# A 1022-operation schedule written out as a list of numbers is replaced by another list

## The chip, the cores and the metric

The kernel runs on one core of a Trainium2 chip. The metric is the device time of one execution in microseconds (us), as the median of several runs; less is better. The core has TensorE (matrix products and transposes, PE in the profile, with its weight loads as PEld), VectorE (DVE), ScalarE (ACT), GpSimd (POOL), SyncE (SP, which here only issues transfers) and 16 DMA engines that all queues share.

## The reference

Two blocks in sequence: an attention with polynomial features, and a wave-MLP over its output.

```python
# q, k, v: (4 batches, 4 heads, 1088 tokens, 32); S1, S2: (8, 32)
phi(x) = outer(S1 x, S2 x)                       # 64 features per token and head
kv  = einsum('bhsf,bhsd->bhfd', phi(k), v)
z   = sum over tokens of phi(k)
x   = (phi(q) kv) / (phi(q) z + 1e-6)            # then (B, H, S, D) -> (4, 1088, 128)
theta = x @ w_theta
zr, zi = x * cos(theta), x * sin(theta)
y   = w_tok_r @ zr + w_tok_i @ zi                # token mixing, 1088 x 1088, per batch
u   = x + y
out = u + relu(u @ w_ch)
```

The weights come as 64-bit words (w_tok, w_sq, S1, S2) and are made into 32-bit numbers on the chip; q, k and v come in 32 bits.

## The kernel before

**Stages.** For each of the four batches b there is a key side (load k and v; transposes kT, features kf, sums kv; a scale from the sum of squares; a rounding "grid" of the keys; key sums), a chain of small operations on the key sums (L.stage "chain", over batch 0, then 1, then 2 and 3 together) that gives the scaled sums in mv and mf, and a query side (load q; qscale; transposes qT scaled on the way; q0, the rounded part, and the rest). Then come, for each batch in order: `levels` (three groups of matmuls with a ScalarE copy of each, line 1002, and the denominator on VectorE), `num_g` for g = 0, 1, 2 (features of the queries on VectorE, transposed by TensorE at line 1064 and copied by ScalarE at 1068, or sent through DRAM for batches 2 and 3; matmul with kv; copy at 1078) and `theta_g` (theta on TensorE, sine and cosine on ScalarE at lines 1115 and 1117, products with x on VectorE, written to z). Below, "num1" is the three num stages of batch 1.

**Token mixing.** The 17 rows of w_tok, 128 x 1088 each, are loaded one by one (1088 KB, line 583), taken to 32 bits by two ScalarE operations (584 and 586) and two on VectorE (309 and 305), and stay in SBUF. Batches 0 and 1 are mixed directly, 17 x 3 matmuls each (128 x 384 per matmul: `mix0`, `mix1`). Batches 2 and 3 share seven products in Winograd's manner (m1 to m7; m5 is the first that needs theta of batch 3). Behind each the output stage adds x, multiplies by w_ch and stores.

**Joins.** A `join` is an accumulating transfer from SBUF to SBUF that GpSimd issues (line 319). In batches 2 and 3 it does the subtraction of a rounded half from the keys (ops 216 and 217 for batch 2, 252 and 253 for batch 3) and from the queries (329, 334); batches 0 and 1 use it in their output stage. The `small` operations of GpSimd, such as pbd, the block of key products that the scale chain's second matmul reads, stand in the same sequence.

**What sets the order.** Each operation is recorded by `op(engine, duration, function, writes, reads)` and gets a number. Nothing is scheduled when the kernel is built: `Layout.run` reads the sequence from the constant ORDER and each buffer's slot from PLACES, and `Layout.issue` walks it under a manual schedule:

```python
        self.order = [self.ops[int(i)] for i in ORDER.split()]
...
        for o in self.order:
            n, home = spins.get(o.i, 0), None
            if shared:
                for _ in range(n):
                    fill()
            for b in o.bufs:
                if b.ap is None:
                    raw = pools[b.cls](b.slot)
...
            o.fn()
```

Each engine, and the queue of each engine that issues transfers (SP, ACT, POOL), executes its own operations in the order in which ORDER names them. A buffer gets its slot at its first use, and waits there until the buffer that held the slot before has been read for the last time; the classes have 22 ("big"), 5 ("zs"), 6 ("hf") slots and so on. A wait on another engine is made by what reads what. SPINS says ahead of which operation `fill` issues how many filler matmuls of 128 x 384 into a PSUM buffer nobody reads (line 379); ten more are issued as operation 1. Operation 3 (line 384) computes one sine on ScalarE whose output, `warm`, nobody reads. The constants' durations in `op` are used for nothing in this kernel, since the order is given.

Matmuls go through `mm` (line 341), VectorE's two-input operations through `tt` (305), its scalar ones through `ts` (309), the combined ones through `stt` (312), so many operations share a line in the profile.

Of the kernel before, what the change touches and what calls it, by code (L numbers as in the profile page):

```python
# [26 lines left out]
TINY = 2.0**-60  # L27
UP = 256.0
ORDER = (
    "6 4 2 5 44 0 1 45 50 3 47 7 340 8 48 46 11 9 10 49 12 29 58 13 30 70 83 84 64 76 71 14 77 85 96 15 88 72 89 78 "  # L30
    "65 86 90 97 79 16 91 66 159 17 92 26 87 98 67 148 27 93 80 32 18 68 19 73 99 309 25 94 141 20 310 74 95 31 142 "
    "35 149 341 21 101 129 151 160 102 150 40 103 104 161 130 105 342 41 131 106 135 107 43 343 162 197 345 136 108 "
    "360 210 22 137 152 355 305 42 53 344 307 198 315 138 306 313 28 110 109 211 139 132 111 23 314 100 308 212 203 "
    "112 133 316 113 36 69 24 204 114 33 199 213 34 143 115 117 75 116 311 144 59 81 200 118 119 312 317 82 346 120 "
    "191 39 121 37 122 124 123 145 424 60 335 125 38 348 422 375 153 420 423 425 154 214 421 155 347 426 61 427 318 "
    "349 246 156 428 57 126 157 239 319 192 158 356 429 227 127 240 164 128 62 247 165 241 430 167 63 337 166 431 "
    "168 249 134 51 432 242 193 169 228 433 140 336 229 170 434 146 194 233 171 350 230 435 173 56 172 147 436 234 "
    "174 361 443 439 437 175 450 438 176 446 440 444 177 441 447 250 445 453 178 442 248 179 448 180 320 454 357 "
    "457 181 188 451 182 338 459 385 458 452 205 183 251 449 235 184 352 460 252 185 187 186 358 521 461 163 339 "
    "462 517 463 253 359 519 518 217 522 455 520 464 236 465 206 523 456 482 524 467 222 215 525 216 351 468 483 "  # L40
    "526 469 353 365 471 527 223 362 473 354 466 189 470 254 528 255 472 529 484 256 190 530 475 387 224 476 257 "
    "376 531 485 267 532 377 268 533 366 390 540 534 370 536 269 537 543 547 541 535 321 542 363 548 270 550 378 "
    "549 538 544 364 386 218 219 368 539 551 388 545 54 220 477 380 201 221 546 552 367 195 325 554 263 553 379 400 "
    "225 486 556 479 264 326 265 389 322 474 266 487 478 557 371 369 558 323 207 196 324 271 372 373 202 480 208 "
    "395 272 562 374 209 381 563 571 382 570 383 488 327 564 405 384 392 489 275 481 391 231 401 410 393 555 490 "
    "560 403 559 273 394 572 396 491 276 274 328 278 573 402 329 492 398 277 565 574 415 404 397 279 406 493 399 "
    "576 280 561 52 407 281 494 282 408 411 409 566 625 575 626 243 567 579 412 413 495 237 283 414 416 496 285 284 "
    "417 418 497 286 299 287 568 419 288 498 55 289 290 293 291 294 292 577 578 648 569 511 505 512 650 649 226 652 "
    "651 627 653 628 654 629 655 602 295 656 580 657 581 658 603 296 604 659 660 582 258 661 583 499 662 300 232 "
    "500 663 238 330 259 506 630 605 298 664 584 260 585 665 261 586 331 262 671 501 666 667 606 513 332 631 333 "  # L50
    "587 678 334 607 502 588 503 589 301 297 514 608 679 609 672 590 632 842 674 668 591 841 673 592 840 681 633 "
    "719 680 721 720 723 722 244 724 669 245 725 610 675 726 670 504 611 727 612 728 593 729 685 686 594 730 688 "
    "595 731 682 302 732 613 687 676 733 634 734 677 614 697 735 635 699 698 615 736 696 596 689 690 839 616 597 "
    "737 691 683 838 692 303 684 636 304 738 742 637 638 708 701 617 743 709 694 693 639 702 707 695 703 700 618 "
    "710 744 749 815 805 704 750 787 705 788 712 816 745 796 640 711 797 798 751 598 706 817 713 739 641 756 714 "
    "799 715 818 789 752 599 790 515 800 844 516 716 819 619 791 718 801 717 620 820 802 746 806 803 807 753 792 "
    "740 808 741 809 760 821 762 810 763 747 845 754 804 748 843 642 811 764 769 755 643 757 822 771 778 765 621 "
    "772 780 758 812 813 622 759 793 781 766 761 768 823 767 773 644 774 794 835 782 770 645 775 846 795 777 847 "
    "776 784 848 783 855 864 856 836 857 814 858 867 779 849 785 859 875 837 868 860 861 866 893 850 876 894 851 "
    "869 884 870 862 885 871 852 872 853 877 865 886 898 887 854 878 895 879 863 888 874 901 880 896 507 873 889 "  # L60
    "938 911 935 890 881 939 882 786 891 824 912 883 902 892 913 940 825 897 903 826 955 646 914 900 915 830 600 "
    "904 942 601 916 831 956 937 957 899 933 975 647 905 934 946 945 931 943 906 907 508 917 509 947 941 510 918 "
    "936 908 827 948 974 958 976 828 959 832 960 932 834 949 944 833 950 829 961 962 951 963 952 987 953 988 954 "
    "919 909 920 989 623 977 990 624 991 926 964 927 978 910 965 992 979 966 921 968 980 922 981 982 928 983 923 "
    "984 925 924 985 930 993 967 986 994 995 969 996 1007 971 929 1012 1013 1014 997 998 1015 999 1008 1000 1001 "
    "1009 1002 1003 1011 1010 1004 1005 970 1006 1016 1017 972 1018 1019 973 1020 1021 "
)
PLACES = (
    "7 0 1 5 0 10 17 16 14 0 15 5 6 15 18 0 10 3 5 0 11 5 3 4 3 6 3 6 2 2 8 4 4 0 5 12 0 6 12 4 12 4 6 5 4 7 1 5 8 "
    "5 10 8 4 4 1 5 9 0 8 8 5 2 0 4 1 6 10 1 0 1 1 4 2 4 0 3 1 4 6 0 4 3 5 1 3 2 21 2 10 6 5 8 3 5 4 3 5 12 4 1 0 2 "  # L70
    "3 2 9 2 0 6 4 4 1 2 1 0 4 2 3 7 3 5 3 3 5 2 4 4 4 6 4 5 4 1 3 5 0 2 3 5 2 0 8 12 1 7 0 7 0 11 4 2 12 7 2 5 5 8 "
    "3 5 3 1 5 4 2 8 12 3 0 3 2 4 3 5 0 1 0 2 4 4 1 7 4 5 3 0 3 19 0 11 13 2 11 8 2 5 16 0 10 2 1 4 7 4 1 11 0 10 3 "
    "4 1 5 3 15 17 1 20 14 1 17 20 3 0 1 4 15 6 0 18 0 1 10 18 3 10 9 0 10 0 6 1 5 6 0 12 2 0 0 0 6 6 2 2 1 4 4 1 0 "
    "7 0 1 6 5 4 1 4 1 4 5 0 0 3 6 5 0 2 4 4 1 3 7 2 0 3 5 4 21 1 21 4 3 4 2 5 7 2 3 7 4 7 1 2 5 2 2 4 7 2 7 1 3 2 "
    "5 4 1 1 0 2 5 3 4 5 4 0 5 5 0 5 2 3 4 6 12 1 3 1 1 2 4 0 2 3 2 3 3 6 5 0 4 1 2 3 0 0 0 6 3 0 0 3 0 7 10 1 10 3 "
    "1 2 2 0 3 1 1 6 3 0 4 5 0 0 3 5 4 6 4 2 6 5 2 5 3 2 0 5 4 15 7 1 6 5 7 0 5 0 1 5 1 6 7 2 6 0 1 7 3 3 1 4 2 5 2 "
)
SPINS = (
    "70:2 15:3 137:1 211:1 424:2 128:1 168:1 174:2 176:1 521:2 "
)  # L80
WARM = 0
SPLIT = ()
# [1330 lines left out]
```

## Time and profile before

| | us |
|---|---|
| device time, median of 3 runs (219.3 to 219.84) | 219.76 |
| span of the profiled execution (no other time of its own is given) | 217.4 |
| TensorE busy | 209.3 |
| of that, 27 fillers (L379) | 7.8 |
| VectorE busy | 181.2 |
| ScalarE busy | 111.2 |
| GpSimd busy | 22.2 |
| 17 rows of w_tok, 1088 KB each, from issue to landing (min, median, max) | 4.9, 7.0, 11.0 |

The page of the profile lists, in this order: busy time and share of each engine; the span in 40 slices of 5.4 us, with a digit per slice for the busy tenths; the DMA queues; the chain of work that ended last, by engine; and the costliest groups of instructions (line, engine, operation, output<-input, partitions x elements, count, then busy time and mean ns of one, then the idle time before them and what ended it). Stretches of the trace list busy time and number of instructions for PE, PEld, DVE, ACT and POOL, the granted clock of TensorE (1.00 is full), the mean share of the 16 DMA engines and GB/s. Timelines list start, duration, engine, line and operation; in brackets the idle time before and what ended it. A VectorE or ScalarE instruction can start before its neighbour has ended, so busy times can overlap.

### The profile page before, as it was taken

What the parts mean: (1) busy time and instruction counts of PE and PEld (TensorE: products, weight loads), DVE (VectorE), ACT (ScalarE), POOL (GpSimd) and SP (SyncE); (2) the same over time, 40 slices, a digit from 0 to 9 for tenths busy, and PEclk for the clock granted to TensorE, in tenths of its full rate; (3) what the DMA queues carried; (4) which work ended last, traced back from release to release, by engine and by line L of the source; (5) the groups of instructions that cost most, each with busy time, mean ns of one, the idle gap of its engine ahead of it and who ended that gap; (6) DMA issues with size and microseconds to landing.
All of it is one profiled execution on the core that took longest, in us unless ns stands there. A gap on an engine that the chain in (4) does not pass through costs nothing.

```text
span 217.4 us, 5063 instructions
## 1 busy us (share of the span) xinstructions
PE 209.3 (96%) x1998; PEld 154.3 (71%) x1998; DVE 181.2 (83%) x408; ACT 111.2 (51%) x214; POOL 22.2 (10%) x44
## 2 busy tenths in 40 slices
PE   7999899999999999999999999999999999999994
PEld 3987786686766686666766575667758788888883
DVE  4899999999999999999599839988138999996542
ACT  3998498899779999983322040354037400000010
POOL 2237000055000000100132000100101000000000
PEclk9999999999999999999999999999999999999998
DMA  5999996869979979894226998599911000045253
GB/s 153 429 406 340 425 399 203 333 224 271 267 276 361 361 264 380 219 198 126 33 36 102 222 137 199 105 156 151 231 78 32 0 0 0 3 66 89 36 79 75
DMA packets 52635, 40.58 MB, mean 187 GB/s; under 512 B 45444, under 2 KB 47108, under 8 KB 50436
## 3 DMA queue, kind: packets, MB, share of 16 engines
q1 hardware_dynamic: 35540, 33.71, 48.7%
q0 software_dynamic: 1728, 4.65, 10.5%
q10 hardware_dynamic: 15344, 1.90, 6.0%
q8 instruction: 15, 0.25, 0.5%
q14 instruction: 8, 0.07, 0.1%
HBM read 30.43 MB, written 5.18 MB: 164 GB/s over the span
## 4 chain that ended last, share of the span: by engine, by line
PE 72%; DVE 12%; ACT 8%; DMA 4%; ACTq 2%; issue 2%; SPq 1%
PE ps L341 66%; DMA big<-q_l 2%; DVE lv L305 2%; PE ps L1064 2%; ACTq L333 2%; PE ps L1098 1%; DMA fx<-g 1%; DVE g L305 1%; DVE big L305 1%; PE ps L967 1%; ACT big L584 1%; ACT big L937 1%; DVE hf L309 1%; DVE zs L305 1%; ACT g L1068 1%
## 5 line engine op out<-in xcount | busy, mean ns | idle before, releaser
L341 PE MATMUL ps<-big,zs 128*128 128x384 f32 (+4 forms) x398 | 109.7, 424 | 0.4 <-DVE zs L305 0.4
L341 PEld LDWEIGHTS ps<-big,zs 128*128 128x128 f32 x398 | 71.4, 190 | 30.3 <-issue 2.6
L1201 ACT COPY g<-ps 128x128 f32<-128x128 f32 (+1 forms) x3 | 0.9, 301 | 42.5 <-PE ps L1193 42.5
L305 DVE CUSTOM_DVE_ANT_0 big<-big,big 128x2176 uint16<-128x2176 uint16 x17 | 21.8, 1287 | 0.4 <-ACT big L586 0.2
L584 ACT ACTIVATE big<-zs 128x1088 f32<-128x1088 f32 x17 | 20.9, 1235 | 2.1 <-DMA zs<-w_tok 1.2
L586 ACT ACTIVATE big<-zs 128x1088 int32<-128x1088 uint32 (+1 forms) x18 | 21.3, 1184 | 0.1
L341 PE MATMUL ps<-big,big 128*64 128x64 f32 (+2 forms) x208 | 20.6, 276 | 0.0
L341 PEld LDWEIGHTS ps<-big,big 128*64 128x64 f32 (+1 forms) x208 | 16.5, 154 | 2.9 <-issue 0.2
L305 DVE TENSOR_TENSOR big<-big,big 128x544 f32<-128x544 f32 x24 | 16.7, 712 | 0.0
L1002 ACT COPY lv<-ps 128x480 f32<-128x480 f32 x12 | 6.3, 563 | 14.2 <-PE ps L341 14.2
L312 DVE SCALAR_TENSOR_TENSOR g<-g,ps 128x384 f32<-128x384 f32 x12 | 6.6, 548 | 8.1 <-ACT g L1111 8.1
L1078 ACT COPY big<-ps 128x384 f32<-128x384 f32 x12 | 5.9, 489 | 14.0 <-PE ps L341 8.3
L309 DVE TENSOR_SCALAR big<-big 128x1088 int32<-128x1088 int32 x17 | 12.2, 724 | 0.6 <-ACT big L584 0.5
L341 PEld LDWEIGHTS ps<-w,big 128*128 128x128 f32 x80 | 10.6, 192 | 2.3 <-ACT g L1068 0.6
L319 POOL DMA_DIRECT2D big<-hf x6 | 5.4, 957 | 63.3 <-DVE g L312 33.8
L319 POOL DMA_DIRECT2D g<-big x6 | 5.2, 920 | 64.8 <-ACT g L1179 34.7
L341 PE MATMUL ps<-w,big 128*128 128x128 f32 x80 | 11.8, 280 | 0.0
L305 DVE TENSOR_TENSOR g<-lv 128x768 f32<-128x768 f32 x12 | 11.2, 945 | 0.0
L341 PE MATMUL ps<-g,sm 128*64 128x384 f32 x48 | 10.1, 507 | 0.2 <-ACT big L1078 0.2
L305 DVE TENSOR_TENSOR zs<-ps,g 128x768 f32<-128x768 f32 (+2 forms) x15 | 9.4, 632 | 1.0 <-PE ps L1098 0.9
L341 PEld LDWEIGHTS <-hf 128*64 128x64 f16 (+1 forms) x288 | 7.7, 110 | 2.9 <-issue 1.7
L379 PE MATMUL ps<-idle 128*128 128x384 bf16 x27 | 7.8, 400 | 1.3 <-POOL idle L381 1.3
(194 smaller groups left out, 336.6 us busy)
## 6 DMA issues: line engine op xcount, KB each, us to landing
zs<-w_tok SPq DMA_DIRECT2D x17, 1088.0 KB, 7.0
big<-k_l SPq DMA_DIRECT2D x6, 576.0 KB, 6.6
big<-hf POOLq DMA_DIRECT2D x6, 576.0 KB, 6.0
big<-v_l SPq DMA_DIRECT2D x4, 576.0 KB, 7.0
g<-fq SPq DMA_DIRECT2D x6, 384.0 KB, 5.2
big<-q_l SPq DMA_DIRECT2D x3, 576.0 KB, 5.1
fq<-g SPq DMA_DIRECT2D x12, 96.0 KB, 4.0
fq<-g ACTq DMA_DIRECT2D x12, 96.0 KB, 4.1
```

Of the source, the lines that this page charges most:

```text
L305: eng.tensor_tensor(out=o, in0=a, in1=b, op=f)
L309: (eng or V).tensor_scalar(out=o, in0=a, scalar1=s1, scalar2=s2, op0=op0, **kw)
L312: (eng or V).scalar_tensor_tensor(out=o, in0=a, scalar=s, in1=b, op0=op0, op1=op1)
L319: op("G", 0.9, lambda: G.dma_start(dst(), src(), accum_op=ALU.add), w, r, fly=fly)
L333: E.dma_start(there().rearrange("(a i) (x b j) -> b i x a j", a=nf, b=nf, j=SQ)[f], blocks()[f * SQ:(f + 1) * SQ].rearrange("i (x a j) -> ...
L341: T.matmul(o, lhs, rhs, start=start, stop=stop, skip_group_check=True)
L379: T.matmul(nowhere() if home is None else view(home, (GW,), F32), idle()[:, 0:P], idle(), start=True, stop=True, skip_group_check=True)
L584: op("A", 0.22 + n * 0.0009, lambda: A.activation(dfn(), words_of(raw(), n)[1].bitcast(F32), AF.Prelu, scale=2.0**-112, alpha=-(2.0**32)), ...
L586: op("A", 0.22 + n * 0.0009, lambda: A.activation(stp(), words_of(raw(), n)[0].bitcast(U32), AF.Copy, scale=2.0**-29), [stp], [raw])
L1002: op("A", act(480), lambda g=g, lp=lp: A.copy(lv().rearrange("p l (c n) -> p l c n", n=HR)[:, :, g * GC:(g + 1) * GC], lp().rearrange("p c ...
L1064: T.transpose(tr()[:, i * P:(i + 1) * P], qp()[:, i * H + 2 * n:i * H + 2 * n + 2].rearrange("p h i j -> p (h i j)"), ident())
L1078: op("A", act(GW), lambda g=g, xp=xp: A.copy(xt()[:, g * GW:(g + 1) * GW], xp()), cells(xt, g * GW, (g + 1) * GW), [xp])
```

## The change

Three constants change and no function does. ORDER names the same 1022 operations in another sequence; 25 of them keep their place. PLACES gives 357 of 419 buffers another slot. SPINS asks for 9 fillers in six places where it asked for 16 in ten. The file is two lines shorter, so a line of the new kernel has a number two lower than here. In numbers that the prediction uses, places counted from 0: operation 3 moves from 9 to 370; the joins 217, 216, 252, 253 from 309, 325, 293, 305 to 93, 109, 135, 163; VectorE's operation of the second group of num1 (540) from 366 to 397. Operation 58 is the load of w2, 0 and 1 are the fillers' buffer and the first ten fillers, 2 writes the constants, 5 and 6 load the S matrices.

```diff
--- before.py
+++ after.py
@@ -27,56 +27,54 @@
 TINY = 2.0**-60
 UP = 256.0
 ORDER = (
-    "6 4 2 5 44 0 1 45 50 3 47 7 340 8 48 46 11 9 10 49 12 29 58 13 30 70 83 84 64 76 71 14 77 85 96 15 88 72 89 78 "
-    "65 86 90 97 79 16 91 66 159 17 92 26 87 98 67 148 27 93 80 32 18 68 19 73 99 309 25 94 141 20 310 74 95 31 142 "
-    "35 149 341 21 101 129 151 160 102 150 40 103 104 161 130 105 342 41 131 106 135 107 43 343 162 197 345 136 108 "
-    "360 210 22 137 152 355 305 42 53 344 307 198 315 138 306 313 28 110 109 211 139 132 111 23 314 100 308 212 203 "
-    "112 133 316 113 36 69 24 204 114 33 199 213 34 143 115 117 75 116 311 144 59 81 200 118 119 312 317 82 346 120 "
-    "191 39 121 37 122 124 123 145 424 60 335 125 38 348 422 375 153 420 423 425 154 214 421 155 347 426 61 427 318 "
-    "349 246 156 428 57 126 157 239 319 192 158 356 429 227 127 240 164 128 62 247 165 241 430 167 63 337 166 431 "
-    "168 249 134 51 432 242 193 169 228 433 140 336 229 170 434 146 194 233 171 350 230 435 173 56 172 147 436 234 "
-    "174 361 443 439 437 175 450 438 176 446 440 444 177 441 447 250 445 453 178 442 248 179 448 180 320 454 357 "
-    "457 181 188 451 182 338 459 385 458 452 205 183 251 449 235 184 352 460 252 185 187 186 358 521 461 163 339 "
-    "462 517 463 253 359 519 518 217 522 455 520 464 236 465 206 523 456 482 524 467 222 215 525 216 351 468 483 "
-    "526 469 353 365 471 527 223 362 473 354 466 189 470 254 528 255 472 529 484 256 190 530 475 387 224 476 257 "
-    "376 531 485 267 532 377 268 533 366 390 540 534 370 536 269 537 543 547 541 535 321 542 363 548 270 550 378 "
-    "549 538 544 364 386 218 219 368 539 551 388 545 54 220 477 380 201 221 546 552 367 195 325 554 263 553 379 400 "
-    "225 486 556 479 264 326 265 389 322 474 266 487 478 557 371 369 558 323 207 196 324 271 372 373 202 480 208 "
...
+    "6 4 0 2 5 58 1 44 48 47 7 49 8 50 11 9 345 10 60 56 12 29 59 45 13 30 14 51 15 57 84 83 76 340 61 16 70 46 62 64 77 "
+    "335 17 210 78 360 85 88 203 355 18 89 25 40 65 53 21 135 71 35 22 204 213 23 86 79 191 136 197 90 246 24 26 137 34 "
+    "32 192 27 87 80 19 91 198 36 211 33 159 92 214 212 249 41 66 217 93 39 67 215 138 148 20 250 31 160 42 94 68 346 95 "
+    "216 139 239 347 72 38 141 161 101 73 102 162 350 348 104 163 240 103 105 307 251 96 227 74 142 106 252 107 222 97 "
+    "151 241 98 43 309 228 108 223 63 109 152 242 110 99 111 310 100 308 305 199 153 306 233 341 253 112 224 113 311 154 "
+    "200 342 143 28 349 69 75 81 225 375 129 114 226 115 149 116 130 343 155 336 117 150 118 312 131 337 156 119 120 82 "
+    "144 121 54 125 361 122 124 123 338 380 422 145 157 420 423 339 132 234 424 421 133 158 425 126 356 235 164 127 321 "
+    "426 325 165 427 357 317 247 128 428 229 236 134 365 166 230 429 140 318 146 167 430 315 322 205 358 168 206 193 431 "
+    "147 326 218 169 432 219 316 170 433 194 254 171 434 220 313 173 221 362 248 435 323 172 436 174 314 370 443 437 439 "
+    "175 450 440 176 444 438 446 177 178 441 447 179 180 344 445 453 324 451 442 188 454 181 263 457 182 452 183 319 458 "
+    "459 455 37 351 460 255 184 320 461 448 463 256 185 187 456 186 264 257 353 521 352 265 359 189 519 462 449 354 517 "
+    "522 520 465 266 464 518 473 467 523 377 466 468 482 190 524 469 475 525 470 483 267 526 471 376 476 527 3 367 484 "
+    "400 472 528 366 529 485 530 477 268 372 531 269 486 532 270 533 371 547 478 385 536 479 534 390 540 474 535 550 537 "
+    "481 548 551 541 368 543 549 538 363 544 542 552 364 381 545 271 373 382 487 369 546 395 539 480 387 555 383 554 378 "
+    "386 488 374 553 405 379 401 563 489 384 556 392 570 195 391 490 557 388 558 415 560 272 389 559 491 402 393 275 397 "
+    "403 410 562 394 492 396 207 406 493 398 201 399 196 202 208 408 411 494 404 407 413 495 564 409 412 273 417 276 496 "
+    "274 414 277 416 565 497 561 566 327 572 209 418 625 278 568 626 328 573 279 329 419 574 579 576 580 280 52 281 498 "
...
 )
 PLACES = (
-    "7 0 1 5 0 10 17 16 14 0 15 5 6 15 18 0 10 3 5 0 11 5 3 4 3 6 3 6 2 2 8 4 4 0 5 12 0 6 12 4 12 4 6 5 4 7 1 5 8 "
...
+    "1 7 1 12 7 18 4 9 11 5 10 14 3 0 17 0 14 13 20 4 19 4 3 3 6 4 0 4 5 0 8 4 2 5 6 9 3 9 0 3 15 4 4 3 5 6 5 5 10 4 8 7 "
...
 )
 SPINS = (
-    "70:2 15:3 137:1 211:1 424:2 128:1 168:1 174:2 176:1 521:2 "
+    "15:1 91:1 105:3 97:2 113:1 422:1 "
 )
```

## The prediction

> **What bounds the kernel now.** I read the shares of the page first, then its 40 slices, the chain that ended last, stretches of ten microseconds, and last the rows of single engines where the new sequence moves most.
>
> ```profile
> PE 209.3 (96%) x1998; PEld 154.3 (71%) x1998; DVE 181.2 (83%) x408; ACT 111.2 (51%) x214; POOL 22.2 (10%) x44
> ...
> DVE  4899999999999999999599839988138999996542
> ...
> DMA  5999996869979979894226998599911000045253
> ...
> PE 72%; DVE 12%; ACT 8%; DMA 4%; ACTq 2%; issue 2%; SPq 1%
> ...
> L379 PE MATMUL ps<-idle 128*128 128x384 bf16 x27 | 7.8, 400 | 1.3 <-POOL idle L381 1.3
> ```
>
> TensorE is busy 96% of the span, but 7.8 us of that are 27 fillers (L379), so its own work is some 201 us. The row of slices says that VectorE is as full as TensorE up to about 100 us and that the DMA engines are full over most of the first 70 us. A full TensorE alone would make any new sequence worthless; the stretches show where it isn't full.
>
> ```profile
> 20.00:30.00 10.00, 9.17 (x275) 8.15 (x276) 9.79 (x31) 6.46 (x14) 0.29 (x2) 1.00 1.01 419
> 30.00:40.00 10.00, 9.00 (x182) 6.86 (x177) 9.90 (x26) 9.09 (x20) 0.00 (x0) 1.00 0.72 249
> 40.00:50.00 10.00, 10.00 (x158) 7.11 (x157) 9.97 (x26) 9.32 (x20) 3.87 (x3) 1.00 0.82 295
> 50.00:60.00 10.00, 10.00 (x102) 7.35 (x103) 9.82 (x22) 8.61 (x16) 2.09 (x3) 1.00 1.05 271
> ```
>
> The columns are PE, PEld, DVE, ACT, POOL, the granted clock, the DMA share and GB/s. From 7 to 65 us VectorE has no gap worth the name: the time at which an operation ends is the VectorE work ahead of it in the sequence plus about 5 us (the offset is 4.6 at 9 us, 5.1 at 25, 5.3 at 60). TensorE loses time only where it catches up with VectorE (0.8 us in 20 to 30, 1.0 in 30 to 40, 0.7 in 60 to 70). So the end is set by a crossing: the moment VectorE finishes what a stage of TensorE needs, plus all of TensorE's work that the sequence leaves behind that point, plus the tail of 3.2 us. At the second group of batch 1's numerator (op 540; num1 below) this comes out in full: VectorE finishes it at 62.8, TensorE is busy for 151.4 behind it, and 62.8 + 151.4 + 3.2 = 217.4, the span. The profile gives no other own time; the median of the runs, 219.76, stands 2.4 above it, and I add 2.4 throughout.
>
> **The change, part by part.** Only the sequence, the slots and the fillers change.
>
> *Neighbours on VectorE.* Two kinds of neighbour can be seen in these rows:
>
> ```profile
> 105.61 0.46 DVE L309 TENSOR_SCALAR big<-lv 128x576 f32<-128x576 f32 x1 [2.64 <-ACT lv L1002]
> 106.10 0.76 DVE L305 TENSOR_TENSOR lv<-lv,big 128x576 f32<-128x576 f32 x1
> ...
> 109.49 0.45 DVE L1016 TENSOR_REDUCE sm<-lv 128x36 f32<-128x288 f32 x1
> 109.85 0.75 DVE L1018 TENSOR_REDUCE sm<-lv 128x36 f32<-128x576 f32 x1
> ```
>
> The second waits for the first and starts 30 ns after its end; the fourth needs nothing of the third and starts 90 ns before its end. Over the whole trace independent neighbours overlap by 83 ns (median of 312), dependent ones stand 35 ns apart: 118 ns for each dependent pair. Counted in the two built programs, VectorE instructions that wait on the one just before them go from 67 to 96. So the change does the reverse of its description on this engine: 29 x 0.118 = 3.4 us more of VectorE, part of it ahead of the crossing.
>
> *The crossings.* Adding the rows' own durations in each sequence, VectorE's work up to the end of num1 grows by 3.0 us, and TensorE's work behind that point shrinks by 5.8 (145.5 to 139.7 without excess), because the transposes, sums and key products of batches 2 and 3 now come earlier. Net -2.8. The other crossings move so: VectorE-ready + work left + tail is 206.4, 210.3, 210.1, 211.2 for the first levels, second levels, first mix, num1 before; after it is 208.9 (first levels), 208.4 (num1), 208.8 (second scale chain), 208.4 (first mix). The largest falls by 2.3. TensorE's rows run longer than these bare figures. With the mean durations of the same rows before comes out at 218.1, after at 217.2 (first levels) and 216.5 (num1): -0.9 overall, -1.6 at num1. So -2.8 and -0.9 are the ends; I take the mean durations, since before they land within 0.7 of the span and the bare ones 6.2 below it.
>
> *The loads.* Before, k0 lands at 5.36 and starts VectorE's main work; now w2 goes ahead of it (first come, at 1.42 us for each 576 KB load in the full queue) and k0 comes at about 6.0, but less is lost on the way to the first chain (4.85 against 5.12): -0.25. Behind these, 1088 KB rows of w_tok come at 2.65 us each, and adding them up in the new sequence gives row 1 at 22.7, row 0 at 26.8, row 5 at 29.4, row 4 at 32.1, wanted by ScalarE at 24.1, 27.1, 29.6, 33.0. There is almost no slack.
>
> *The joins.* Four accumulating transfers that GpSimd issues (ops 217, 216, 252, 253) move from places 293 to 325 of the sequence to 93 to 163.
>
> ```profile
> big<-hf POOLq DMA_DIRECT2D x6, 576.0 KB, 6.0
> ...
> 46.13 1.06 POOL L319 DMA_DIRECT2D big<-hf  x1 [25.84 <-DVE mv L878]
> ...
> 49.45 1.78 POOL L319 DMA_DIRECT2D big<-hf  x2
> 52.08 0.85 POOL L319 DMA_DIRECT2D big<-hf  x1 [0.84 <-DVE hf L309]
> ```
>
> Each holds all 16 engines for 2.45 us, 9.8 in all, and they move from 48 to 58 us into about 14 to 24 us, where the DMA share is 1.01. What they cost there depends on who goes first. Row 10, issued at 44.6, kept the engines until 48.7 although a join was ready at about 47.6; and a join ready first was served ahead of row 6, which landed 9.0 us after its issue and held ScalarE:
>
> ```profile
> 62.61 1.23 ACT L584 ACTIVATE big<-zs 128x1088 f32<-128x1088 f32 x1 [1.20 <-DMA zs<-w_tok]
> ```
>
> That is service in order of arrival. By it one join (217, ready at 14.6) is ahead of row 5, which then lands at 31.9: 2.3 us later than wanted, of which VectorE has 1.2 in hand: +1.1 at the first denominator. The wait stands on ScalarE's own queue; behind it are the level copies that VectorE reads. Bounds: 0 (no join ready by then) and the 7 to 8 us of the first rival. On GpSimd the small pbd operation that the first scale chain needs stands behind joins 216 and 252, which cost 0.85 to 1.2 us each to issue; if their inputs are in time this is hidden under VectorE's first 25 us.
>
> The Trainium skill, "DMA: Bandwidth & Descriptors", section "Queues, rings and completion order", says instead that each engine takes turns between the queues that have work, a packet at a time. By that rule the rows would share the engines with all four joins, which is the first rival; the row 10 and join 216 rows speak against it.
>
> *The activation table.* The warm-up (op 3) goes from place 9 to 370.
>
> ```profile
> 1.58 1.28 ACT L384 ACT_TABLE_LOAD   x1 [1.58 <-DVE hm L366]
> ```
>
> It pulled the sine's table in while ScalarE was idle. Built, the new program loads one table at its start and a second ahead of the first sine (first theta stage), near 50 us, where ScalarE is 86 to 93% busy. ScalarE's margin against VectorE is about 1.8 us there before and less behind row 5; 1.28 us turns into a VectorE wait of 0.7 to 1.1 ahead of num1. I take 0.9; 0 if ScalarE has slack left, 1.3 if none.
>
> The Trainium skill, "ScalarE: Activation LUTs", section "What ACT_TABLE_LOAD costs", puts a switch at 2.66 us with the drain; by that this term would be about 2.1 and the forecast 221.1. The row agrees with its load alone and shows no drain, since nothing ran before it.
>
> *Fillers and slots.* 27 fillers become 20. Where they stand TensorE waits anyway (ten run before the first load lands); the shorter warm-up is bounded by the clock, granted at 1.00 in all stretches above: 0. Slots: no buffer in the new sequence becomes free later than its next writer by the same sums; 0, with 0.3 either way. The late part (m5 to the end) has 0.1 us of margin before and after: 0.
>
> *Sum, at num1:* -1.6 - 0.25 + 1.1 + 0.9 = +0.15 on mean durations, against the 218.1 that they give for before; the first levels (217.2) stay below. Span 217.55, time **219.9**. With bare durations it is -2.8 - 0.25 + 2.0 = -1.05 or 218.7; with the terms' upper ends 221.5.
>
> **The rivals.**
>
> 1. *Joins and loads interleave* (the other side). Place: rows 1, 0, 5, 4 on SP's queue at 14 to 42 us. Price: the four joins' 9.8 us spread over the loads; row 1 at 27.6, row 0 at 34.2, row 5 at 39.3, so the first denominator waits 7 to 8 us on VectorE, 6 more than in the forecast: **225.8**. It decides once row 5 lands after about 33. For: full DMA share, no slack. Against: the two cases of service by arrival above.
> 2. *The table and the dependent waits cost more.* Five crossings now lie within 0.5 us of each other, so each late microsecond anywhere counts; with 2.1 for the switch and 1 us of further waits at the crossings (before, TensorE lost 2.5 us at them from 20 to 70): 219.9 + 1.2 + 1 = **222.1**. For: ScalarE is 9.3 of 10 there. Against: VectorE's gapless rows hide ScalarE's delays of up to 1.8.
> 3. *The plan's gain arrives.* Rows land in time and the table falls into slack: only -2.3 counts, 219.76 - 2.3 = **217.5**. For: the same offset of 5 us all along VectorE. Against: joins in a full DMA stretch.
> 4. *The change doesn't do what it says*: already counted, 67 to 96 waits.
>
> **How the numbers follow.** About 0.3% (0.66 us) is what a measurement can tell from none, so "same" is 219.1 to 220.4. Forecast 0.44, own range 218.4 to 221.5: 0.13 below, 0.16 in, 0.15 above. Rival 1 0.25, rival 2 0.14, both slower; rival 3 0.17, faster. So faster 0.30, same 0.16, slower 0.54. The range takes in all but part of the outer cases: 217.3 to 226.0.
>
> **What would show it.** In the new profile: a second table load before the first L1117 or L1115 sine near 50 us; joins issued between 13 and 24 us; row 5's activation (L584) released by DMA 2 us late, with a VectorE gap behind it; the first levels' matmuls starting at about 30.5 instead of 25.2; num1 ending at about 67.5 instead of 62.8 with some 146.8 us of TensorE work behind. It is wrong if rows land after 33 us (rival 1), if TensorE, not VectorE, is late at num1, or if the late part, taken at nothing, opens gaps behind 100 us.

## The result and the profile after

| | before | after |
|---|---|---|
| device time, us (median of 4) | 219.80 | 229.97 (229.66 to 231.58) |
| span of the profiled execution, us | 217.4 | 228.1 |
| TensorE busy, us | 209.3 | 213.5 |
| VectorE busy, us | 181.2 | 184.6 |

The kernel got slower by a ratio of 1.049 (95% interval 1.044 to 1.054), some 10.2 us, and lies outside the range that was given. Medians here and below are of all runs of a kernel; ratios leave out runs that took over 1.5% longer than its fastest. The page of the changed kernel, in the lines that answer to those shown of before (its helpers' lines have numbers two lower):

```profile
PE 213.5 (94%) x1991; PEld 160.2 (70%) x1991; DVE 184.6 (81%) x408; ACT 113.0 (50%) x215; POOL 22.2 (10%) x44
...
DVE  4858797679979999999769895689957899989523
...
PEclk9999999889999999999999999999999999999999
DMA  5999999999003698900982999277796330100043
...
zs<-w_tok SPq DMA_DIRECT2D x17, 1088.0 KB, 8.7
...
big<-hf POOLq DMA_DIRECT2D x6, 576.0 KB, 10.3
big<-v_l SPq DMA_DIRECT2D x4, 576.0 KB, 17.7
```

VectorE now has holes from the third slice to the twelfth (5, 8, 7, 9, 7, 6, 7, 9, 9, 7 where there were nines), the DMA engines are full for nine slices without a break, and the median time from issue to landing has gone from 6.0 to 10.3 us for the joins and from 7.0 to 17.7 for v. The granted clock shows a dip, over two slices, that before did not have. The chain that ended last is no help here: its account breaks off at 158 us. The stretches of ten microseconds of the changed kernel (PE, PEld, DVE, ACT, POOL, granted clock, DMA share, GB/s):

```profile
20.00:30.00 10.00, 8.57 (x107) 6.81 (x104) 8.52 (x28) 9.67 (x24) 3.16 (x4) 1.00 1.05 348
30.00:40.00 10.00, 8.43 (x286) 7.96 (x284) 8.28 (x21) 5.49 (x10) 2.36 (x3) 1.00 1.04 366
40.00:50.00 10.00, 8.45 (x185) 7.07 (x183) 6.54 (x16) 8.09 (x19) 0.00 (x0) 0.83 1.02 425
50.00:60.00 10.00, 9.71 (x151) 7.67 (x147) 9.68 (x29) 7.93 (x18) 0.00 (x0) 1.00 0.72 286
60.00:70.00 10.00, 8.65 (x138) 6.84 (x134) 8.48 (x17) 9.64 (x20) 0.00 (x0) 1.00 0.01 2
```

Before, VectorE was busy for 9.7 to 10.0 of 10 here. Now, but for 50 to 60 us, neither VectorE nor TensorE is full; both wait for something else.

The crossing at num1 splits the loss in one step. VectorE's second operation of num1 (op 540) ends at 77.8 us instead of 62.8, and from there to the end of the span it takes 150.3 instead of 154.6. So the new sequence did gain some 4 us behind that point, as TensorE's work moved ahead of it, and lost 15 on the way to it. I use three marks of that kind below, ends of VectorE operations in the trace: the last of the first scale chain (op 124), the last of the first denominator (435) and op 540. "Planned" is the prediction's own sum: VectorE's accumulated work plus 4.85 us, plus 1.1 from the denominator on and 0.9 more at num1.

| end of, us | op 124 | op 435 | op 540 |
|---|---|---|---|
| before | 25.1 | 38.5 | 62.8 |
| planned for after | 30.4 | 42.7 | 67.5 |
| after, measured | 35.4 | 52.2 | 77.8 |
| late against the plan | 5.0 | 9.5 | 10.3 |

Half of the loss lies ahead of the first scale chain's end, nearly all the rest between it and the first denominator's.

**Who shares the DMA engines.** The rows of w_tok reach ScalarE late, and each holds what stands behind it on that queue:

```profile
34.82 1.20 ACT L582 ACTIVATE big<-zs 128x1088 f32<-128x1088 f32 x1 [1.61 <-DMA zs<-w_tok]
...
39.76 1.18 ACT L582 ACTIVATE big<-zs 128x1088 f32<-128x1088 f32 x1 [2.43 <-DMA zs<-w_tok]
```

These are rows 0 and 5, which I had planned for 27.1 and 31.9. The queues' shares of 25 to 28 us (packets, MB, share of the 16 engines), first of after, then of before in 53 to 55, while its joins ran:

```profile
q0 software_dynamic: 108, 0.49, 62.4%
q1 hardware_dynamic: 109, 0.49, 43.0%
```

```profile
q0 software_dynamic: 129, 0.52, 105.5%
```

With loads and joins both queued the engines take 108 packets of the one and 109 of the other: they take turns. In the other stretches of three microseconds from 22 to 37 us it is 75 to 94 packets of joins beside 91 to 120 of loads, so both go on all the time, if not always one for one. The Trainium skill, "DMA: Bandwidth & Descriptors", section "Queues, rings and completion order", states that rule, and in the stretch of 25 to 28 us the trace agrees. The four joins, which land 2.1 to 2.7 us apart when they are alone, stretch from 20 to 40 us, and the loads get the rest. In the old kernel a join had the engines to itself because the one load issued meanwhile had not begun: row 6, issued at 53.6, sends its first packet at 57.2, and from then on the two queues share, as the stretch of 57 to 59 shows. Why it took 3.6 us to begin isn't shown.

```profile
q0 software_dynamic: 53, 0.19, 62.8%
q1 hardware_dynamic: 32, 0.28, 33.6%
```

### The profile page after: what moved, and what is told of

Read it like the earlier page. It is cut to its first block, busy times and chain, and to the rows that moved or that the text cites. A ratio compares the mean times of both kernels' runs of the same rounds, so it can differ in the third digit from the quotient of the medians.

```text
span 228.1 us, 5059 instructions
## 1 busy us (share of the span) xinstructions
PE 213.5 (94%) x1991; PEld 160.2 (70%) x1991; DVE 184.6 (81%) x408; ACT 113.0 (50%) x215; POOL 22.2 (10%) x44
## 5 line engine op out<-in xcount | busy, mean ns | idle before, releaser
L339 PE MATMUL ps<-big,zs 128*128 128x384 f32 (+4 forms) x398 | 108.5, 423 | 1.4 <-DVE zs L303 1.4
L339 PE MATMUL ps<-big,big 128*64 128x64 f32 (+2 forms) x208 | 21.6, 292 | 0.0
L1199 ACT COPY g<-ps 128x128 f32<-128x128 f32 (+1 forms) x3 | 0.9, 301 | 38.3 <-DMA out<-g 31.9
L339 PEld LDWEIGHTS ps<-big,big 128*64 128x64 f32 (+1 forms) x208 | 17.5, 169 | 3.0 <-issue 0.4
L1109 ACT ACTIVATE g<-ps 128x384 f32<-128x384 f32 x12 | 5.7, 483 | 15.8 <-DMA fq<-g 7.3
L317 POOL DMA_DIRECT2D big<-hf x6 | 5.5, 920 | 79.6 <-ACT g L1115 73.9
L339 PE MATMUL ps<-g,sm 128*64 128x384 f32 x48 | 9.5, 499 | 0.0
L339 PE MATMUL ps<-mf,big 128*64 128x96 f32 x144 | 8.2, 249 | 0.6 <-DMA big<-hf 0.6
L303 DVE TENSOR_TENSOR g<-sm,ps 128x768 f32<-128x768 f32 x6 | 5.6, 951 | 3.6 <-ACT sm L753 3.6
## 6 DMA issues: line engine op xcount, KB each, us to landing
big<-hf POOLq DMA_DIRECT2D x6, 576.0 KB, 10.3
big<-v_l SPq DMA_DIRECT2D x4, 576.0 KB, 17.7
```

The lines of the kernel that those rows point to most:

```text
L303: eng.tensor_tensor(out=o, in0=a, in1=b, op=f)
L317: op("G", 0.9, lambda: G.dma_start(dst(), src(), accum_op=ALU.add), w, r, fly=fly)
L339: T.matmul(o, lhs, rhs, start=start, stop=stop, skip_group_check=True)
L1109: op("A", act(GW), lambda cs=cs, th=th: A.activation(cs()[:, 0], th(), AF.Copy, bias=ROUND), [(cs, 0)], [th])
L1199: op("A", act(w), lambda: A.copy(ot(), ut()), [ot], [ut])
```

## The experiments

The kernels of the new sequence scatter by 1.2 to 7.0 us from run to run. In the traces' records of the granted clock each dip ahead of the last microseconds lasts 3.413 us or two or three times that, at half speed. Every run of the old kernel has a mean clock of 0.997 or more. A run's mean clock leaves out a cold start, of which there is no record. Times below are medians of four runs unless said; the old kernel beside them had 219.3 to 219.9.

**e1: joins that move next to nothing.**

```diff
-            join(rc, lambda: flat(kn()), [r], [kn])
+            join(lambda: rc()[:, 0:32], lambda: flat(kn())[:, 0:32], [r], [kn])
-            join(kc, lambda: flat(kb()), [kx], [kb])
+            join(lambda: kc()[:, 0:32], lambda: flat(kb())[:, 0:32], [kx], [kb])
```

> The four joins of the keys (ops 216, 217, 252, 253) move 32 columns instead of 1152, so their keys are not rounded off and the output is wrong; waits, order and every other operation stay. Theory J (joins and loads share the engines): rows 1, 0, 5, 4 land near 24, 27, 30, 33 us instead of 27.4, 34.8, 39.7, 42, the first levels no longer wait behind row 0 on ScalarE, and the time falls by 4 to 6 us, to 224 to 226. Rival W (a cold TensorE delays the first scale chain): chain 0 still ends near 35, the levels start no earlier than 36, and the time falls by less than 2 us.

227.42 us, ratio 1.028 (1.023 to 1.032). The four runs are 225.0 and 226.0 with the clock at 1.0, and 228.9 and 232.0 at 0.982 and 0.985. The ratio is that of the first two. In the profile, of the run of 232.0, row 0 lands at 29.6 instead of 34.8 (theory J had it near 27). The two runs at full clock are 4 to 5 us better, the other two gain 1 us or nothing. And the first scale chain still ends at 35.7, with TensorE at half speed until 19.9. So the joins' bytes cost up to 4 or 5 us, the dips that go with them included, and something else holds the chain.

**e2: fillers that keep TensorE fed from the start.**

```diff
 SPINS = (
-    "15:1 91:1 105:3 97:2 113:1 422:1 "
+    "15:4 91:1 105:3 97:2 113:1 422:1 "
```

> Four fillers instead of one stand ahead of the first ScalarE-dependent matmul (op 15), so TensorE is fed from 1.3 to about 6.5 us. Theory W: the clock is granted in full at about 6 us instead of 19.7, the matmuls from 7 to 19 us take half as long, chain 0 ends 3 to 4 us earlier, near 31 to 32; the time falls by 3 to 5 us. Theory J: the clock rises as in W, but row 0 still lands at 34.8 and ScalarE's copy behind it still holds the first levels, so the time falls by less than 2 us.

229.97, ratio 1.048 (1.043 to 1.053): nothing. Yet the clock did what W said. The same nine transposes, in the old kernel, in the changed one and in e2:

```profile
5.41 1.20 PE L739 MATMUL ps<-ident,big 128*128 128x128 f32 x9 [0.23 <-DMA big<-k_l]
```

```profile
6.87 2.18 PE L737 MATMUL ps<-ident,big 128*128 128x128 f32 x9
```

```profile
6.73 1.21 PE L737 MATMUL ps<-ident,big 128*128 128x128 f32 x9
```

In the profiled execution of after TensorE runs at half speed until 19.7 us, where its first record of the full clock begins; in e2 until 4.9. The profile's clock column doesn't show this: it gives 1.00 where there is no record. In e2 another wait is next, and it is one that the prediction had named and put at nothing. Its GpSimd rows, and the matmul of the scale chain that reads pbd:

```profile
26.58 0.89 POOL L317 DMA_DIRECT2D big<-hf  x1 [6.95 <-DMA big<-k_l]
27.20 0.72 POOL L303 TENSOR_TENSOR pbd<-psc,hm 128x128 f32<-128x128 f32 x1
```

```profile
27.97 1.06 PE L339 MATMUL ps<-sm,pbd 128*128 128x32 f32 x4 [2.68 <-POOL pbd L303]
```

GpSimd waits 6.95 us to issue join 252, whose target r3, a load of batch 3's keys, is still landing, and pbd stands behind it. TensorE idles, the clock is at half from 25.3 to 35.6, and chain 0 ends at 38.5, later than in after.

**e3: the warm-up sine back at the start.**

```diff
-    "6 4 0 2 5 58 1 44 48 ...  476 527 3 367 484 ...
+    "6 4 0 2 5 3 58 1 44 48 ...  476 527 367 484 ...
```

> Only the warm-up sine (op 3) is moved back to the start, so the second table load is gone. My term: 0.7 to 1.1 us less. With the page's 2.66 us for a switch: about 2 us less. If other waits cover it: within 0.4 us of the changed kernel.

229.71, ratio 1.045 (1.040 to 1.049): 0.3 us, less than the runs scatter. The wait that the late load causes is real and goes away: in after TensorE stands for 1.35 us at 62.2 behind it, in e3 it doesn't. The time doesn't show it. (The clock came up at 5.3 us in this profile with the single filler of after, and chain 0 ended at 36.5, held by pbd as in e2.)

**e4: the old kernel without its early fillers.**

```diff
 SPINS = (
-    "70:2 15:3 137:1 211:1 424:2 128:1 168:1 174:2 176:1 521:2 "
+    "137:1 211:1 424:2 128:1 168:1 174:2 176:1 521:2 "
```

> The old kernel without the five fillers ahead of ops 70 and 15. Theory W (early fillers get the clock up): the clock rises later than 4.6 us, by one to four windows of 3.4 us, and the kernel gets 1 to 4 us slower. Rival (the window happened to lie well): the ten fillers at the start suffice, the clock is full at 4.6 us again and the time stays within 0.5 us of 219.8.

219.64 (ten runs), ratio 1.001 (0.999 to 1.004). The initial fillers suffice: in the profiled execution the clock is full at 4.8 us. Two of the ten runs are at 220.9 and 221.4.

**e5: joins late.** The four numbers move in ORDER, nothing else does:

```diff
-    ... 66 217 93 ...  95 216 139 ...  106 252 107 ...  233 341 ... 253 112 ...
+    ... 122 217 124 216 123 338 ...  325 252 165 ... 253 ...
```

> The changed kernel with only the four joins moved back in the sequence: 217 and 216 from places 93 and 109 to the end of the first scale chain (near 35 us), 252 and 253 from 135 and 163 to the first denominator (near 43 us); every transfer keeps its size. Theory J: no join lies among the loads of 14 to 35 us, so rows 1, 0, 5, 4 land near 23, 27, 30, 33, pbd is not held on GpSimd, the first levels start 3 us or more earlier, and the time falls by 4 to 6 us, to 224 to 226. Theory W (half-speed TensorE early and after 40 us is the cause): the time falls by less than 2 us.

226.96, ratio 1.032 (1.027 to 1.036); the run with the clock at 1.0 has 225.7. Rows 0 and 5 are taken up at 33.3 and 35.8, and pbd is made at 24.2. Chain 0 still ends at 35.6: TensorE is at half speed until 20.0 us in this profile, which is of the slowest run (231.2). With the joins early and TensorE warm (e2) the chain is late, and with the joins late and TensorE cold (here) it is late too, so taking away one shows little.

**e6: e5, e2 and e3 together.**

> Joins moved back as in e5, four fillers ahead of op 15 as in e2, and the warm-up sine back at the start as in e3. If joins, cold clock and table are the whole loss: chain 0 ends near 31, no clock drop, and the time is 217 to 219. If the waits in the late part (1.4 us at the second Winograd product) and the dependent neighbours count as well: 219 to 222. If the loss lies elsewhere: above 225.

225.55, ratio 1.025 (1.017 to 1.033), best run 223.0. Chain 0 ends at 30.8, where the plan had 30.4. So the first 5 us are explained: a cold TensorE (e5) and pbd behind the joins (e2), side by side. But op 435 ends at 45.4 and op 540 at 73.1, still 2.7 and 5.6 late.

**e7: fillers in the waits of after** (4 ahead of op 15, 4 of 223, 12 of 111, 6 of 422, 5 of 158).

```diff
-    "15:1 91:1 105:3 97:2 113:1 422:1 "
+    "15:4 91:1 105:3 97:2 113:1 422:6 111:12 158:5 223:4 "
```

> The changed kernel with more fillers where TensorE waits: 4 ahead of op 15, 4 ahead of 223, 12 ahead of 111, 6 ahead of 422, 5 ahead of 158; the joins stay early. If the drops of the granted clock cost time by themselves: no drop from 5 us on, and the time falls by 3 to 4 us, to 226 to 227. If they are only a sign of the waits: within 1 us of the changed kernel.

230.67, ratio 1.051 (1.048 to 1.054). Two runs have the clock at 0.999 and 1.0 throughout and take 230.7 and 231.7. While the joins are early, filling the dips gains nothing. The 29 fillers more, 0.33 us each, take time of TensorE's own, so it isn't shown that the dips cost nothing.

**e8: the old kernel with a late table load.**

```diff
-    "6 4 2 5 44 0 1 45 50 3 47 7 340 ...
+    "6 4 2 5 44 0 1 45 50 47 7 340 ...   (3 stands ahead of 367)
```

> The old kernel with only the warm-up sine (op 3) moved behind the first theta stage, as the change has it, so that a second table load of 1.28 us comes ahead of the first sine near 50 us. My term: 0.7 to 1.1 us slower. With the page's 2.66 us: about 2 us slower. If ScalarE has slack there: within 0.4 us of the old kernel.

220.10 (ten runs), ratio 1.0013 (0.9996 to 1.0029): 0.3 us, not told from nothing. The load itself:

```profile
47.65 1.28 ACT L1114 ACT_TABLE_LOAD   x1
48.95 0.62 ACT L1114 ACTIVATE g<-g,halfpi 128x384 f32<-128x384 f32 x1
```

It starts as the work before it ends (47.09 + 0.55) and the sine starts 0.02 us behind it. The Trainium skill, "ScalarE: Activation LUTs", section "What ACT_TABLE_LOAD costs", adds a drain of 1.38 us; in these rows there is none to see.

**e9: loads later in the sequence.** Rows 3, 8, 9, 6 and v of batch 2 (ops 350, 375, 380, 365, 54) moved behind op 219.

> e6 with five loads that nothing needs before 55 us (rows 3, 8, 9, 6 and v of batch 2) moved on SP's queue behind the issue of batch 2's key products (rest2). Theory F (in e6 TensorE stops for 0.9 to 1.9 us at every 256th of its instructions because its own program is fetched through the same busy DMA engines, and the moved joins land late for the same reason): the DMA share from 33 to 43 us falls, the joins land by 42, the stops at instructions 1217 and 1473 shrink to under 0.4 us, and the time falls by 2 to 4 us below e6, to 220 to 222. Rival (the stops are the fetch's own rate, whatever the DMA engines do): they stay at 1 to 2 us each and the time stays above 223. Third: the deferred rows land after 58 us and ScalarE waits for them, which gives back what was won.

224.69, ratio 1.022 (1.016 to 1.027), but the edit did nothing: SP had those loads at the same times, as these rows of its queue show, first of e6, then of e9.

```profile
20.06 7.84 SPq L582 DMA_DIRECT2D zs<-w_tok  x2
30.82 0.33 SPq L613 DMA_DIRECT2D big<-v_l  x1
```

```profile
20.35 8.11 SPq L582 DMA_DIRECT2D zs<-w_tok  x2
31.41 0.33 SPq L613 DMA_DIRECT2D big<-v_l  x1
```

A queue runs ahead until something that it needs is missing; a later place in a list that all engines share delays nothing. (It holds for the joins too: e6 issues them at 28.5 to 30.4, not at 35 to 43.) So e9 is e6 a second time, and 0.9 us is what two such medians differ by. Its profile, with the clock full throughout, shows what is left. TensorE's rows with idle time that no wait explains:

```profile
32.84 0.34 PE L378 MATMUL ps<-idle 128*128 128x384 bf16 x1 [1.47 <-issue]
...
39.22 0.38 PE L966 MATMUL ps<-ident,big 128*128 128x128 f32 x2 [0.95 <-issue]
...
45.41 0.41 PE L340 MATMUL ps<-hf 128*64 128x64 bf16 x14 [1.86 <-issue]
```

The last one lies in the middle of one operation's matmuls. Counting TensorE's instructions in the trace (matmuls, weight loads and the 47 semaphore and drain instructions between them), the three stops come at numbers 962, 1217 and 1473, some 256 apart, and in the variants that have such stops they come at these numbers and at 3265, seven times 256 further on. The page's DMA queue "instruction" moves 16 KB packets, 15 in a run, one for each 256 of TensorE's 4,000 instructions, and the stops end 1.4 to 1.5 us after such a packet has landed (1.25 to 1.6 in e6). TensorE has run out of program: I found nothing else in the traces that fits both the distance and the landings. The old kernel and the changed one have no such stop; in the changed one TensorE comes to the same places later than its program does.

**e10: e9 with one store earlier.** Op 504 moved ahead of op 680 on SP's queue.

> e9 with the store of the first output third (op 504) moved one place up on SP's queue, ahead of the last transposing transfer of num2 (680). The first theta of batch 2 (op 686) waits for the slot of that store's source; with it 2.7 us of VectorE wait and 1.3 us of TensorE wait at the second Winograd product. If the late part cost time as the gap shows: 0.8 to 1.3 us less than e9. If another wait stands behind it: no change.

224.91, ratio 1.021 (1.015 to 1.027). In e9 VectorE stands still for the slot of that store's source:

```profile
137.99 0.58 DVE L325 STREAM_TRANSPOSE g<-big 128x384 f32<-128x384 f32 x1 [2.69 <-DMA out<-g]
```

In e10 this wait and TensorE's 1.35 us at the second Winograd product are gone; the time isn't lower. One stop for program (0.55 us, at instruction 3265) has come in ahead of it, and the profiled run has two dips of the clock.

**e11: e9's sequence without the fillers and with the late table load.**

> The changed kernel with the joins late (as e5) and the five loads deferred (as e9), but the fillers and the late table load as the change has them. If transfers are the whole cause: as e9 within 0.7 us. If the cold clock early and the table load count once the transfers are out of the way: 1 to 3 us slower than e9.

227.10, ratio 1.033 (1.026 to 1.040), 2.4 us more than e9. So with the joins later, fillers and table together do count. Chain 0 ends at 31.5, since the clock came up at 5.5 in this profile, with the single filler of after. Up to there this kernel does what e5 does, whose profiled run was cold until 20.0 and had this mark at 35.6: the late clock alone makes some 4 us at the mark. A dip at 46.4 and the 1.36 us wait at the table come ahead of op 540, which ends at 74.9.

**e12: loads really held.** A 16-byte transfer per partition that needs a late VectorE result stands ahead of them in ORDER and on SP's queue.

```diff
+    held = far.tile([P, 4], F32, tag="held", name="held")
+    op("S", 0.1, lambda: SY.dma_start(held, kg[3]()), [], [])
     L.run()
```

> e9 with a tiny transfer added on SP's queue (16 bytes per partition, from the scale constants of batch 3, which VectorE writes near 42 to 45 us) ahead of the loads of row 3, row 8, v of batch 2, row 9 and row 6; SP's queue now really waits there, which a later place in the sequence alone did not do (in e9 these loads were issued at the same times as in e6). Theory F: from 38 to 45 us the joins have the DMA engines to themselves, land by 42, and TensorE's stops at instructions 962, 1217 and 1473 (4.3 us in e9) fall to 1 to 2 us in all; the time falls to 221 to 223. Rival (the fetch has its own rate whatever the DMA engines do): the stops stay at 4 us and the time at 224 to 225. Third: row 3 lands after 55 and ScalarE waits, no gain.

224.70, ratio 1.027 (1.019 to 1.034): no faster, but it answers the question. The stretch of 40 to 45 us of e9 and then of e12, and e12's stops:

```profile
40.00:45.00 5.00, 3.55 (x123) 3.03 (x124) 3.76 (x11) 3.11 (x9) 0.00 (x0) 1.00 1.05 341
```

```profile
40.00:45.00 5.00, 4.15 (x132) 3.46 (x133) 3.53 (x8) 2.59 (x9) 0.00 (x0) 1.00 0.35 89
```

```profile
34.14 0.34 PE L378 MATMUL ps<-idle 128*128 128x384 bf16 x1 [1.41 <-issue]
...
40.79 0.38 PE L966 MATMUL ps<-ident,big 128*128 128x128 f32 x2 [1.22 <-issue]
```

With the DMA share at 0.35 the third stop is gone, and program packets start 3.4 and 3.9 us apart (38.5, 42.0, 45.9) where e9 has 6.1 and 6.2 (36.9, 43.0, 49.2). The first two lie where the joins alone keep the share above 1.0, and stay. So in these two profiles the fetch is slower where the engines are busier. The 1.7 us that are saved don't show in the time. All four runs have a mean clock near 0.992, and in the profiled one a dip from 24.8 to 28.2 goes with the end of the first scale chain at 32.6 instead of 31.4.

**e13: e12 and the early store.**

> e12 with the store of the first output third moved up on SP's queue as in e10. If the gap of 1.3 us ahead of the second Winograd product is on the path that sets the end: 0.7 to 1.3 us less than e12. If TensorE only meets another wait or stop behind it, as e10 against e9 would have it: within 0.5 us of e12.

222.70, ratio 1.013 (1.007 to 1.018), best run 221.1; the best version of the new sequence, and still slower than the old one. Against e12 it is 2.0 less, but its clock is better; between runs of clock 0.992 the difference is 0.8 us and more (223.1 and 223.5 against 224.3, 224.4 and 227.4). So the store seems to count here, where in e10 it didn't show.

**e14: small joins, fillers and early table.**

> The changed kernel with the joins early but moving 32 columns instead of 1152 (as e1; the keys of batches 2 and 3 are not rounded off), with the fillers of e2 and the early table load of e3. It is the new sequence without the joins' bytes, without the cold start and without the late table. If joins, clock and table are the whole loss: 217 to 219. If TensorE's own program fetch takes the rest: 3 to 5 us of stops at its instructions 962, 1217 and 1473 and 221 to 223.

225.00, ratio 1.025 (1.020 to 1.029). The joins' bytes, the cold clock and the table together make 5 of the 10 us. In this profile are left 3.6 us of program stops, pbd again behind join 252 (op 43 ends at 25.5 and TensorE waits 1.36 us for it), a dip from 26.1 to 29.5, and the late store; what each of them costs isn't told apart.

The marks again, in us, with the profiled execution of each:

| | op 124 | op 435 | op 540 |
|---|---|---|---|
| planned | 30.4 | 42.7 | 67.5 |
| after | 35.4 | 52.2 | 77.8 |
| e2, warm clock alone | 38.5 | 52.1 | 79.6 |
| e5, joins late alone | 35.6 | 51.2 | 80.3 |
| e6, joins late, warm, table early | 30.8 | 45.4 | 73.1 |
| e9, the same again | 31.4 | 45.9 | 72.2 |
| e12, loads held too | 32.6 | 47.5 | 72.4 |
| e13, store early too | 31.0 | 46.3 | 71.3 |

From op 540 to the end of the span it is 149.1 to 150.4 us in all of these, 154.6 in the old kernel. In e13, op 540 is 3.8 us later than planned, and the two stops ahead of it make 3.2 (1.74 and 1.49).

## Why the prediction was wrong, step by step

The step that failed is the price of the joins, +1.1 by service in order of arrival: the queues share the engines, rows of w_tok came up to 8 us late, and the joins' bytes were worth up to 4 or 5 us (e1). With it failed two terms put at nothing, the fillers and pbd, and a term that no step had, TensorE's program.

- *What bounds the kernel* held: the time is op 540's end plus what TensorE has behind it. The forecast of the second part, 146.8 + 3.2, came out at 150.3, by some luck: TensorE has only 144.2 us of work behind op 540, and stands idle for 3.0 in between (150.6 and 0.8 in the old kernel, which the prediction counted together as 151.4 of work). The first, 67.5, came out at 77.8, and the whole error of the sum lies there.
- *Neighbours on VectorE* held: +3.4 us forecast, 181.2 to 184.6 measured. In the traces the neighbours that start less than 60 ns behind the other's end, by 34 ns in the median, went from 80 to 110, 30 more where 29 had been counted; the others overlap by 84 and 82 ns. The durations add up to 204.5 and 204.4 us, so the lost overlap is all of it.
- *The crossings* held as a sum of work. That each late microsecond would come through, as five crossings lie close together, fits too: op 540 was 10.3 us late against the plan, the kernel 10.1 above the forecast.
- *The joins: service in order of arrival* failed. Packets of the two queues take turns. The rows of before that I read as a line at a counter showed transfers that had not yet begun: row 6, issued at 53.6, has its first packets at 57.2 while the joins run to 60.5, and the join issued at 46.1 has its first at 48.7 while row 10 runs to 49.1. The first rival had the mechanism, its place and its landings: row 1 at 27.6, row 0 at 34.2, row 5 at 39.3, the last by 42, against 27.4, 34.8 and, as ScalarE takes up rows 5 and 4, 39.8 and 42.9. That its 225.8 isn't far from 229.97 doesn't make it whole: it had nothing of the cold start, of pbd or of the program. I gave it 0.25 and should have given it the most, since the Trainium skill ("DMA: Bandwidth & Descriptors", the section named above) stated the rule and the two cases against it were one transfer each.
- *Fillers at nothing* failed. I read the clock column's 1.00 as granted, and the duration of the same nine transposes was the number to ask for. Why the start of after stayed cold isn't shown: e4, of the old sequence, has no filler at this place and was warm at 4.8. Of the eight kernels of the new sequence with four fillers ahead of op 15, each had a full clock by 7.1 us; of the five with one, two at 5.3 and 5.5 and three at 19.7 to 20.0 (one profiled execution each).
- *pbd hidden under VectorE's first 25 us* failed as soon as TensorE was warm (2.68 us in e2). The condition was in the text, and the landing of r3 (the load that join 252 waits for), on which it hangs, came at 22.6 in after and 26.1 in e2.
- *The table at 0.9* was too much: 0.3 in either kernel, not told from nothing. The 2.66 of the Trainium skill, "ScalarE: Activation LUTs", section "What ACT_TABLE_LOAD costs", was farther off.
- *The late part at nothing* failed: in after TensorE waits 2.5 us in three places from 137 to 156, 1.36 of it behind the store's slot, and putting that store earlier was worth 0.8 us or more (e13).
- What no step had: TensorE's own program. With joins, clock and table put right it stopped for 3.6 to 4.4 us (e14, e6), and neither came near the 217.5 of rival 3. None of the variants was free of all its stops, so that they alone keep it out of reach isn't shown.

The range ended at 226.0 because each rival was priced alone. The joins (6 us) and further waits could come together; with the cold start and pbd they did.

What stays open: how the 10 us divide between joins and cold clock, as each hides behind the other up to the first scale chain's end; where the last 3 us of e13 come from; and how much of the scatter from run to run is the clock and how much the transfers. Slots were not tried by themselves.

## What to carry to other kernels

When transfers move into a stretch in which the DMA engines are already full, price them by sharing, not by a line at a counter, and add the bytes wanted by each deadline over all queues. Before calling a queue's step hidden, look at what the instruction ahead of it on that queue waits for; a place in a common list holds nothing back by itself. When a sequence packs many small matmuls into a short time, count TensorE's instructions per microsecond as well as its work.

## What the runs showed of the hardware

- TensorE's program comes in 16 KB packets of 256 instructions through the DMA engines. With a DMA share near 1.0 packets followed each other at 6.1 to 6.5 us in e6 and e9, with 0.35 at 3.4 to 3.9, and TensorE stood 0.65 to 2.1 us at every 256th instruction when it was faster than that. The Trainium skill, "Runtime: NRT & Kernel Launch", section "Instruction fetch mechanics", calls the crossing of such a block mostly hidden; in the old kernel it is, in twelve of the variants the stops sum to 1.5 (e3) to 5.6 us (e5).
- The clock went to half in after (43.6 to 47.1) though TensorE's longest idle time since 30 us was 1.57 us. The Trainium skill, "TensorE: Matmul & The Clock Gate", section "Part 1: The HAM clock gate", has it fall after an idle window of about 3.4 us; the length of the dips agrees (3.413), the idle time here was in pieces.
- Joins of 576 KB that have the engines to themselves land 2.1 us apart (e12: 37.1, 39.3, 41.4, 43.4) and 2.1 to 2.7 in the old kernel, where the prediction took 2.45; loads of the same size land 1.42 apart (7.15, 8.57, 9.99 in the old kernel). In a full stretch the first packet of join 217 came 4.9 us after its issue (14.9 to 19.8).
